# Sixteen key blocks of attention scores in six runs instead of seven, value products in groups of 4, 6 and 6

## The chip, the cores and the metric

The kernel runs on one core of one Trainium2 chip. The metric is the device time of one execution in microseconds (us); lower is better. TensorE (PE) does matrix products, ScalarE (ACT) exponentials and other table functions, VectorE (DVE) elementwise work, GpSimd (POOL) a few helpers; SyncE (SP) issues most DMAs. Each engine takes its own instructions in program order, and semaphores hold an instruction back until what it needs is there.

## The reference

The input x has 2048 tokens of 640 features. Two blocks read the same layer-normed xn, and their results are added to x:

```python
def _A_ref(x, wqkv, wo):              # H = 32 heads of Dh = 20
    q, k, v = qkv[0], qkv[1], qkv[2]  # from x @ wqkv
    scores = einsum("bhqd,bhkd->bhqk", q, k) * (Dh ** -0.5)
    p = _softmax(scores, axis=-1)
    o = einsum("bhqk,bhkd->bhqd", p, v)
    return o.transpose(...).reshape(B, S, D) @ wo

def _B_ref(x, w1, b1, w2, b2):        # F = 1536
    y = _layernorm(x, axis=-1)
    h = _gelu(y @ w1 + b1)
    return h @ w2 + b2

xn = _layernorm(x, axis=-1)
return x + _A_ref(xn, A_wqkv, A_wo) + _B_ref(xn, B_w1, B_b1, B_w2, B_b2)
```

## The kernel before

**Stages.** A first stage (to about 184 us of the profile) normalises x, projects queries, keys and a part of the values. The attention stage follows, and fills nearly all of the rest; what it leaves is the last part of the output projection.

**Tiles of the attention stage.** The heads go in 16 pairs, the queries in two halves of two chunks of 512. One pair and one chunk is a *tile* here; there are 64, numbered from 0, and each goes over 16 *key blocks* of 128 keys, numbered 0 to 15. For each block, `scores` (line 790) makes two matmuls side by side, one for each head of the pair, on 61 rows each, into one of three PSUM buffers, and ACT takes the exponential of the 128x1024 result into `p` (line 792). A next score waits until the exponential three blocks back has left its buffer.

**Value products.** `pv` (line 822) multiplies `p` by the values, four products of 32 columns side by side (a *wave*). A block goes in one of two ways, by the table `SPLIT`. For a 1, the upper 16 bits of `p` are multiplied as they are (one wave for a block), and the remainder, which DVE makes (`rest`, line 804, tile `low`), is multiplied in another wave for two blocks. For a 0 the float32 `p` is multiplied whole, two blocks in one wave of two passes. Inside a group the order is fixed:

```python
for kb, up, _ in split:                 # first the upper halves
    ...
for i in range(0, len(whole), 2):       # then the whole blocks, by twos
    ...
for i in range(0, len(split), 2):       # last the remainders, by twos
    for a in range(2):
        for n, (kb, _, low) in enumerate(split[i : i + 2]):
            product(2 * a + n % 2, vhalf, of16(kb, a), low[:, a])
```

So a group can't end before the remainder of its last split block is there.

**Other work.** Everything else that PE has to do (values, both layers of the second block, the output projection) is a generator `fill`, from which pieces are taken between the runs of scores: first-layer products `pu` (line 1083, a product is 30 matmuls and often falls in two pieces of 15), second-layer products `py` (line 1118), late values `pz`, projection `z`. After a `pu` product DVE and ACT compute the gelu: DVE lines 1014, 1016, 1018, 1020, then tanh on ACT (line 1025), then DVE lines 1027, 1028, 1029. The first of them, line 1014, reads `pu` and is issued with the last matmuls of the product; the others are issued at the following *ticks*, up to some 2 us of work in each. The row-sum divisions and their DVE lines 961 to 1004 (`finish`) come in ticks as well.

**The order.** It is written out by hand in `PLAN`: the rows are walked for each tile, and each word emits its work on all engines at that place.

- `s` the scores and the exponential of the next block
- `v4` or `v6` the value products of the oldest 4 or 6 blocks not yet multiplied (in the first row those are the previous tile's last 4)
- `l3` the remainder of block 3 on DVE, if the block is split
- `t`, `r` a tick (with `r`, tanh may be held back one tick)
- `m` a piece of other work, as much as the next number of `RATE` gives credit for
- `e` the copy of the previous tile's result out of PSUM on ACT (line 847)

After the second row the loads of the next tile's queries and keys are added to the ticks; they go on SP's queue.

Of the kernel before, what the change touches and what calls it, by code (L numbers as in the profile page):

```python
# [23 lines left out]
VW = DH + 1  # L24
PAD = 32 - VW
VROW = H * VW + PAD
SPLIT = (1, 1, 0, 0, 1, 1, 0, 0, 1, 1, 0, 0, 1, 1, 0, 0)
NPAIR = H // 2
EPS = 1e-5
TOP = 15.5  # L30
# [2 lines left out]
KROW = 32768.0  # L33
GRP = 4
CHUNK = 2.1
RATE = (2.0, 1.4, 2.2)
PLAN = ('s s t v4 l0 e', 's s l1 t s r m', 's s t v4', 's s l4 r l5 l8 m', 's s t l9 s r v4', 's l12 s m l13', 's r s v4')
UNITS = (3, 3, 3, 3, 2, 2)
ENDS = tuple(sum(UNITS[: i + 1]) for i in range(len(UNITS)))
TAIL = 12  # L40
# [8 lines left out]
def mha_mlp_kernel(tc, x, wqkv, wo, w1, b1, w2, b2, out):  # L49
# [4 lines left out]
    with (  # L54
# [124 lines left out]
        with tc.tile_pool(name="pa", bufs=2) as pa, tc.tile_pool(name="pa1", bufs=1) as pa1, tc.manual_schedule():  # L179
# [36 lines left out]
            for kb in range(NKB):  # L216
                if SPLIT[kb]:
                    nc.gpsimd.memset(V16[:, kb, :, DH : DH + 1], 1.0)
# [212 lines left out]
            def vproj_out(c, j, ps):  # L431
                kb = 4 * c + j
                pv_ = ps[:, :, :320].rearrange("p f (h d) -> p f h d", d=DH)
                vs = (V16 if SPLIT[kb] else V32)[:, kb].rearrange("p (f h) d -> p f h d", f=2)
                nc.scalar.activation(vs[:, :, :, :DH], pv_, AF.Copy, scale=2.0**-14)
                if SPLIT[kb]:
                    nc.vector.scalar_tensor_tensor(vs[:, :, :, VW : VW + DH], pv_, 2.0**-14, vs[:, :, :, :DH],
# [172 lines left out]
            def head_values(c, ps):  # L610

                for j in range(4):
                    kb = 4 * c + j
                    pv_ = ps[:, j // 2, j % 2 * VC :][:, :VC].rearrange("p (h d) -> p h d", d=DH)
                    vs = (V16 if SPLIT[kb] else V32)[:, kb, :VH]
                    nc.scalar.activation(vs[:, :, :DH], pv_, AF.Copy, scale=2.0**-14)
                    if SPLIT[kb]:
                        nc.vector.scalar_tensor_tensor(vs[:, :, VW : VW + DH], pv_, 2.0**-14, vs[:, :, :DH],
# [91 lines left out]
        with ExitStack() as scope:  # L710
# [88 lines left out]
            def rest(unit):  # L799

                kb, pt = unit[3:]
                if SPLIT[kb]:
                    low = ptp.tile([P, 2, 512], F16, tag="low", name="low", bufs=4)
# [486 lines left out]
            with tc.manual_schedule():  # L1290
# [15 lines left out]
                def other(turn):  # L1306

                    nonlocal credit
                    if not runs:
                        unit = next(fill)  # L1310
                        if unit is None:
                            credit = 0.0
                            return
                        n, cost = unit
                        lens, have = [], credit
                        while not lens or (cost - have > 0.5 * RATE[(turn + len(lens)) % len(RATE)] and len(lens) < n):
                            if lens:
                                have += RATE[(turn + len(lens)) % len(RATE)]
                            lens.append(max(0.0, have))
                        cuts = [round(n * v / lens[-1]) for v in lens] if lens[-1] > 0 else [n]  # L1320
                        runs.extend(y - x for x, y in zip([0] + cuts, cuts))
                    for _ in range(runs.pop(0)):
                        credit -= next(fill)

                for g, hf, cc in flow:
                    units = []
                    turn = 0
                    for r, steps in enumerate(PLAN):
                        for step in steps.split():
# [7 lines left out]
                            elif step == "m":  # L1337
                                credit += RATE[turn]
                                other(turn)
                                turn = (turn + 1) % len(RATE)  # L1340
                            elif step == "e":
# [5 lines left out]
                            else:  # L1347
                                now = int(step[1:])
                                if prev[0] is units[0] and r == 0:
                                    credit += RATE[0]  # L1350
                                    other(0)
# [121 lines left out]
```

## Time and profile before

| what | value |
|---|---|
| median of 3 runs | 1326.81 us (1326.32 to 1327.2) |
| span of the profiled execution | 1325.0 us |
| PE busy | 1313.6 us, 99% |
| ACT busy | 1117.6 us, 84% |
| DVE busy | 1067.1 us, 81% |

The span is the time from the first to the last instruction of the execution that the profiler recorded, so it is 1.8 us under the median of the runs; that execution's whole time is not given apart from its span. The page's busy shares are averages over the whole span. PE's matmuls overlap in the records, each with a modelled end, so the time that a run of matmuls costs is read as the distance from its first start to the next run's first start.

### The profile page before, as it was taken

How to read it: one execution, taken by the hardware profiler on the slowest of the kernel's cores; microseconds unless marked ns; L12 is line 12 of the kernel's file. 1: busy time of each engine (PE TensorE's matmuls, PEld its weight loads, DVE VectorE, ACT ScalarE, POOL GpSimd, SP SyncE). 2: the span in 40 equal slices, each digit the busy share in tenths (PEclk: the TensorE clock that was granted, in tenths of full speed). 3: DMA queues.
4: the chain of work that ended last, by engine and by line, in shares of the span. 5: the costliest groups of instructions: out<-in, count | busy, mean ns of one | idle time of the engine just before them, and what ended most of it. 6: DMA issues, size and time to landing. Idle time of an engine off the chain costs nothing.

```text
span 1325.0 us, 29048 instructions
## 1 busy us (share of the span) xinstructions
PE 1313.6 (99%) x11636; PEld 603.1 (46%) x11636; DVE 1067.1 (81%) x1450; ACT 1117.6 (84%) x1306; POOL 36.0 (3%) x84
## 2 busy tenths in 40 slices
PE   9999999999999999999999999999999999999998
PEld 6454564333444444444444444444444444444366
DVE  7668569798698987889988798998889899998742
ACT  7745369999999999999999999999999999999900
POOL 2000000000000000000000000000000000000000
PEclk9999999999999999999999999999999999999999
DMA  8697631121233321042312124132122333342376
GB/s 308 218 277 206 192 106 35 39 66 54 66 76 100 90 59 52 27 119 68 100 46 61 40 67 119 51 84 58 49 71 81 87 92 89 106 128 80 107 218 191
DMA packets 108166, 135.28 MB, mean 102 GB/s; under 512 B 24308, under 2 KB 74376, under 8 KB 107900
## 3 DMA queue, kind: packets, MB, share of 16 engines
q1 hardware_dynamic: 104588, 125.99, 31.6%
q0 software_dynamic: 2816, 6.90, 2.7%
q8 instruction: 92, 1.51, 0.5%
q10 hardware_dynamic: 624, 0.51, 0.1%
q14 instruction: 46, 0.38, 0.1%
HBM read 86.64 MB, written 43.74 MB: 98 GB/s over the span
## 4 chain that ended last, share of the span: by engine, by line
PE 90%; DVE 5%; ACT 3%; issue 1%; DMA 1%; SPq 0%; POOL 0%; ACTq 0%; DVEq 0%
PE o L822 31%; PE s L790 20%; PE py L1118 12%; PE pu L1083 12%; PE qkp L352 5%; PE z L1260 5%; PE pz L1162 2%; ACT p L792 2%; PE vp L425 1%; DVE st L263 1%; DVE qkhl L368 1%; ACT wv L476 1%; DVE xt L278 1%; ACT junk L101 0%; DVE low L804 0%
## 5 line engine op out<-in xcount | busy, mean ns | idle before, releaser
L792 ACT ACTIVATE p<-s 128x1024 f32<-128x1024 f32 x1024 | 967.9, 1047 | 55.1 <-PE s L790 53.0
L804 DVE TENSOR_TENSOR low<-p 128x1024 f16<-128x1024 f32 x512 | 610.5, 1220 | 123.1 <-ACT p L792 122.4
L822 PE MATMUL o<-p,vfull 128*32 128x512 bf16 (+1 forms) x4096 | 383.6, 493 | 0.0
L790 PE MATMUL s<-qs,ks 61*128 61x512 f16 x2048 | 304.4, 381 | 1.9 <-ACT p L792 1.3
L790 PEld LDWEIGHTS <-ks 61*128 61x128 f16 x2048 | 76.4, 94 | 237.0 <-issue 217.5
L1083 PE MATMUL pu<-xm,w1t 128*128 128x256 f16 x1440 | 172.3, 273 | 0.0
L1118 PE MATMUL py<-w2t,hT 128*128 128x320 f16 x1152 | 170.3, 300 | 1.2 <-DVE xb L1045 0.9
L1083 PEld LDWEIGHTS <-w1t 128*128 128x128 f16 x1440 | 133.8, 98 | 47.4 <-issue 33.0
L822 PEld LDWEIGHTS <-vfull 128*32 128x32 f16 x3072 | 60.1, 95 | 178.2 <-issue 178.0
L1118 PEld LDWEIGHTS <-hT 128*128 128x128 f16 x1152 | 106.3, 98 | 70.3 <-issue 32.6
L352 PE MATMUL qkp<-xnt,wv 128*128 128x512 f16 x600 | 131.4, 379 | 1.5 <-DVE qkhl L368 0.8
L822 PE MATMUL o<-low,vfull 128*32 128x512 f16 x1024 | 100.3, 378 | 0.0
L352 PEld LDWEIGHTS <-wv 128*128 128x128 f16 x600 | 58.1, 98 | 71.2 <-DVE qkhl L368 1.3
L822 PEld LDWEIGHTS o<-p,vfull 128*32 128x32 f32 x2048 | 61.5, 108 | 58.1
L1260 PE MATMUL z<-w1t,ot 128*128 128x320 f16 x480 | 66.9, 299 | 0.0
L1260 PEld LDWEIGHTS <-ot 128*128 128x128 f16 x480 | 46.2, 98 | 21.3 <-issue 3.7
L1217 DVE SCALAR_TENSOR_TENSOR acc<-z,sc,acc 128x320 f32<-128x320 f32 x32 | 17.6, 549 | 38.4 <-PE z L1260 37.6
L367 ACT ACTIVATE qkhl<-qkp,qks 128x1024 f16<-128x1024 f32 (+1 forms) x24 | 23.2, 965 | 29.5 <-PE qkp L352 18.8
L368 DVE SCALAR_TENSOR_TENSOR qkhl<-qkp,qks,qkhl 128x1024 f16<-128x1024 f32 (+1 forms) x24 | 26.5, 1105 | 25.4 <-ACT qkhl L367 25.3
L1108 POOL DMA_DIRECT2D xb<-in_B_b_dram x16 | 13.8, 863 | 1021.3 <-DMA xb<-in_A_x_dram 390.3
L847 ACT ACTIVATE ev<-o 128x512 f32<-128x512 f32 x64 | 38.6, 603 | 2.5 <-PE o L822 2.4
L1162 PE MATMUL pz<-hv,xm 128*128 128x480 f16 x180 | 39.9, 367 | 0.0
(205 smaller groups left out, 726.3 us busy)
## 6 DMA issues: line engine op xcount, KB each, us to landing
qkscr<-qkhl SPq DMA_DIRECT2D x40, 256.0 KB
opart<-ev SPq DMA_DIRECT2D x124, 80.0 KB
ks<-qkscr SPq DMA_DIRECT2D x120, 80.0 KB
xm<-xscr SPq DMA_DIRECT2D x13, 640.0 KB
qs<-qkscr SPq DMA_DIRECT2D x192, 40.0 KB
oa<-opart SPq DMA_DIRECT2D x32, 240.0 KB
xt<-in_A_x_dram SPq DMA_DIRECT2D x16, 320.0 KB
xscr<-xnt SPq DMA_DIRECT2D x4, 1280.0 KB
```

What stands on the lines that cost most here:

```text
L352: nc.tensor.matmul(ps[:, i, :], wv[:, k, q, a, mm * P : (mm + 1) * P], xnts[c][:, k, b, :], start=(k + n == 0), stop=(k == KD - 1 and n == 2))
L367: nc.scalar.activation(hl[:, 0, i0:i1], ps[:, i0:i1], AF.Copy, scale=a)
L368: nc.vector.scalar_tensor_tensor(hl[:, 1, i0:i1], ps[:, i0:i1], a, hl[:, 0, i0:i1], ALU.mult, ALU.subtract)
L790: nc.tensor.matmul(ps[:, a, :], ks[64 * a : 64 * a + 61, kb * P : (kb + 1) * P], qs[64 * a : 64 * a + 61, cc * 512 : (cc + 1) * 512], star ...
L792: nc.scalar.activation(pt, ps, AF.Exp, scale=QS)
L804: nc.vector.tensor_sub(low, pt, upper(pt))
L822: nc.tensor.matmul(pv.o[32 * q : 32 * q + 32, :], src[:, v0 - PAD * (1 - q % 2) :][:, :32], t, start=q not in pv.begun, stop=last, skip_gr ...
L847: nc.scalar.activation(evs[g, hf][:, cc], o, AF.Copy)
L1083: nc.tensor.matmul(ps[:, i], w1v[:, k, (f + i) // 4, a, fo_ : fo_ + P], xnt[:, k, b, :], start=(n == 0), stop=(n == 3 * KD - 1))
L1118: nc.tensor.matmul(ps[:, :320], hTs[mc][:, f, a, j * P : (j + 1) * P], w2v[:, f, b, hf * 320 : (hf + 1) * 320], start=(n == 0), stop=(n == ...
L1162: nc.tensor.matmul(ps[:, : D - VC], feats[c][:, k, a, j * P : (j + 1) * P], hv[:, k, b, :], start=(n == 0), stop=(n == 3 * KD - 1))
L1260: nc.tensor.matmul(ps[:, :320], ot[:, k, a, j * P : (j + 1) * P], wov[:, k, b, h * 320 : (h + 1) * 320], start=(n == 0), stop=(n == 3 * KD ...
```

## The change

Three tables of numbers change, and no line of the code that reads them:

```diff
-SPLIT = (1, 1, 0, 0, 1, 1, 0, 0, 1, 1, 0, 0, 1, 1, 0, 0)
+SPLIT = (1, 1, 0, 1, 1, 0, 1, 0, 0, 1, 0, 0, 1, 1, 0, 0)
...
-RATE = (2.0, 1.4, 2.2)
-PLAN = ('s s t v4 l0 e', 's s l1 t s r m', 's s t v4', 's s l4 r l5 l8 m', 's s t l9 s r v4', 's l12 s m l13', 's r s v4')
+RATE = (2.0, 1.5, 2.1)
+PLAN = ('s s t s v4 l0 e', 's l1 t s r m', 's l3 s t s l4 v6', 's s l6 t s r m', 's l9 t s v6', 's s l12 t s l13 m')
```

Scores go in runs of 3, 2, 3, 3, 2, 3 blocks instead of 2, 3, 2, 2, 3, 2, 2. Value products go in groups of 4 (the previous tile's blocks 12 to 15), 6 (blocks 0 to 5) and 6 (blocks 6 to 11) instead of four groups of 4. Eight blocks are split in both, but other ones: 0, 1, 3, 4, 6, 9, 12, 13 instead of 0, 1, 4, 5, 8, 9, 12, 13. A tile has three pieces of other work and eight ticks in both.

The first place is PE in tile 21, from the first remainders to the next scores. Before, the group ends with the remainders of blocks 0 and 1 (`low_6974`, `low_6987`):

```order
L822 LDWEIGHTS vfull_89
L822 MATMUL o_7026<-low_6974,vfull_89 32x512
L822 LDWEIGHTS vfull_89
L822 MATMUL o_7026<-low_6987,vfull_89 32x512
L822 LDWEIGHTS vfull_89
L822 MATMUL o_7026<-low_6974,vfull_89 32x512
L822 LDWEIGHTS vfull_89
L822 MATMUL o_7026<-low_6987,vfull_89 32x512
L790 LDWEIGHTS ks5_6335
L790 MATMUL s_7044<-qs5_6334,ks5_6335 128x512
```

Now, after the second head's remainders of blocks 0 and 1 (`low_6976`, `low_6984`), those of blocks 3 and 4 (`low_7019`, `low_7033`) stand ahead of the next scores:

```order
L822 MATMUL o_7035<-low_6976,vfull_89 32x512
L822 LDWEIGHTS vfull_89
L822 MATMUL o_7035<-low_6984,vfull_89 32x512
L822 LDWEIGHTS vfull_89
L822 MATMUL o_7035<-low_7019,vfull_89 32x512
L822 LDWEIGHTS vfull_89
L822 MATMUL o_7035<-low_7033,vfull_89 32x512
L822 LDWEIGHTS vfull_89
L822 MATMUL o_7035<-low_7019,vfull_89 32x512
L822 LDWEIGHTS vfull_89
L822 MATMUL o_7035<-low_7033,vfull_89 32x512
L790 LDWEIGHTS ks5_6335
```

The products with block 4's remainder moved one group forward: before, they stood in the tile's third group, after block 11's scores; now they stand before block 8's.

The second place is DVE in the same tile, from block 0's remainder on. Before, the remainders there are `low_6974` (block 0), `low_6987` (1), `low_7053` (4), `low_7056` (5):

```order
L1027 SCALAR_TENSOR_TENSOR u_6844<-w_6845,u_6844 128x512
L1028 TENSOR_SCALAR hT_5966<-u_6844,sc_91 128x2x256
L1029 SCALAR_TENSOR_TENSOR hT_5966<-u_6844,sc_91,hT_5966 128x2x256
L804 TENSOR_TENSOR low_6974<-p_6943 128x1024
L804 TENSOR_TENSOR low_6987<-p_6948 128x1024
L1014 TENSOR_TENSOR u_7011<-pu_6897,r2f_4261 128x512
L1016 TENSOR_TENSOR u_7011<-u_7011,b1t_94 128x512
L1018 TENSOR_TENSOR w_7012<-u_7011 128x512
L804 TENSOR_TENSOR low_7053<-p_6990 128x1024
L1020 SCALAR_TENSOR_TENSOR w_7012<-w_7012,u_7011 128x512
L804 TENSOR_TENSOR low_7056<-p_7014 128x1024
```

Now they are `low_6976` (block 0), `low_6984` (1), `low_7019` (3), `low_7033` (4):

```order
L804 TENSOR_TENSOR low_6976<-p_6942 128x1024
L804 TENSOR_TENSOR low_6984<-p_6947 128x1024
L1027 SCALAR_TENSOR_TENSOR u_6867<-w_6868,u_6867 128x512
L1028 TENSOR_SCALAR hT_5990<-u_6867,sc_91 128x2x256
L1029 SCALAR_TENSOR_TENSOR hT_5990<-u_6867,sc_91,hT_5990 128x2x256
L1014 TENSOR_TENSOR u_7011<-pu_6926,r2f_4289 128x512
L804 TENSOR_TENSOR low_7019<-p_6979 128x1024
L1016 TENSOR_TENSOR u_7011<-u_7011,b1t_94 128x512
L1018 TENSOR_TENSOR w_7012<-u_7011 128x512
L804 TENSOR_TENSOR low_7033<-p_6990 128x1024
```

The end of the previous gelu moved from ahead of block 0's remainder to behind block 1's, and the start of the next one now stands around block 3's remainder, ahead of block 4's. Nowhere does either kernel have more or fewer matmuls, exponentials or remainders than the other.

## Prediction, made before the changed kernel was run

> **What bounds the kernel now.** I read the page first, then PE's waits, then the long middle of the attention stage, then single tiles in the order of time.
>
> ```profile
> span 1325.0 us, 29048 instructions
> PE 1313.6 (99%) x11636; PEld 603.1 (46%) x11636; DVE 1067.1 (81%) x1450; ACT 1117.6 (84%) x1306; POOL 36.0 (3%) x84
> PEclk9999999999999999999999999999999999999999
> ...
> PE 90%; DVE 5%; ACT 3%; issue 1%; DMA 1%; SPq 0%; POOL 0%; ACTq 0%; DVEq 0%
> ```
>
> PE is busy 99% of the span and holds 90% of the chain that ended last. Who waits for whom:
>
> ```profile
> PE s L790 <- ACT p L792: 1.3, 5, 0.5
> DVE low L804 <- ACT p L792: 122.4, 121, 4.2
> ACT p L792 <- PE s L790: 53.0, 109, 2.1
> ```
>
> Columns are total us, times, longest. PE waits 1.3 us in the whole run for exponentials, and no row has it waiting for a remainder. ACT waits 53.0 us for scores: PE sets the pace. In the middle of the stage (busy us of PE, weight loads, DVE, ACT, POOL, then clock):
>
> ```profile
> 360.00:1150.00 790.00, 789.38 (x7462) 346.87 (x7455) 683.84 (x816) 748.88 (x843) 12.02 (x14) 1.00 0.27 74
> ```
>
> PE 789.4 of 790.0, ACT 748.9 (95%), DVE 683.8 (87%). So a tile gets shorter only if PE's own chain does, and ACT and DVE have 5% and 13% of room on average. Whether they have it at the moment at which PE asks is the question of this change.
>
> **What it takes away: switches.** These are PE's starts around two groups, some from narrow windows (start, then modelled length):
>
> ```profile
> 601.97 1.52 PE L1118 MATMUL py<-w2t,hT 128*128 128x320 f16 x10
> 603.42 0.61 PE L790 MATMUL s<-qs,ks 61*128 61x512 f16 x4
> 603.96 0.42 PE L822 MATMUL o<-p,vfull 128*32 128x512 bf16 x4
> 604.20 0.84 PE L822 MATMUL o<-p,vfull 128*32 128x512 bf16 x8
> 604.42 1.04 PE L822 MATMUL o<-p,vfull 128*32 128x512 f32 x8
> 604.85 0.61 PE L822 MATMUL o<-p,vfull 128*32 128x512 f32 x4
> 605.28 0.40 PE L822 MATMUL o<-low,vfull 128*32 128x512 f16 x4
> 605.61 0.61 PE L790 MATMUL s<-qs,ks 61*128 61x512 f16 x4
> ...
> 607.79 0.82 PE L790 MATMUL s<-qs,ks 61*128 61x512 f16 x6
> 608.55 2.35 PE L1118 MATMUL py<-w2t,hT 128*128 128x320 f16 x16
> ```
>
> Two blocks of scores cost 603.96 - 603.42 = 0.54, three 608.55 - 607.79 = 0.76: 0.22 for a block and 0.10 for each run. A group of 4 costs 605.61 - 603.96 = 1.65: upper waves 0.24 and 0.22, a whole wave 2 x 0.43, and 0.33 for the remainders, which is 0.11 over a block's 0.22, since the next matmul is of another kind. Per tile before: 16 x 0.22 + 7 x 0.10 + 4 x 1.65 = 10.82. After: 16 x 0.22 + 6 x 0.10 = 4.12; the group of 4, 1.65; blocks 0 to 5, four upper waves 3 x 0.24 + 0.22 = 0.94, one whole 0.86, two of remainders 0.22 + 0.33, together 2.35; blocks 6 to 11, 0.46 + 2 x 0.86 + 0.33 = 2.51. Sum 10.63. Saved: 0.19 a tile, 64 x 0.19 = 12 us.
>
> One price here is in no row: a wave of remainders behind another. Its bounds are 0.22 (a block inside its run) and 0.33 (as if kinds changed); the second would leave 64 x 0.08 = 5 us. I take 0.22, because two upper waves, the nearest row, follow at 0.24. [...]
>
> The other edits of this kind are worth nothing: three pieces of other work a tile with credit 5.6 both times, eight ticks both times, eight split blocks, the same DMAs behind the same second row. PE's work on them fills the same time wherever it is cut.
>
> **What it adds: a wait for block 4's remainder.** In the group of blocks 0 to 5 the second wave of remainders is due soon after the first piece of other work, and DVE has other instructions ahead of it. Tile 21 before:
>
> ```profile
> 540.43 0.85 PE L790 MATMUL s<-qs,ks 61*128 61x512 f16 x6
> 541.21 1.81 PE L1083 MATMUL pu<-xm,w1t 128*128 128x256 f16 x15
> 542.95 0.64 PE L790 MATMUL s<-qs,ks 61*128 61x512 f16 x4
> ...
> 543.06 0.69 DVE L1014 TENSOR_TENSOR u<-pu,r2f 128x512 f32<-128x512 f32 x1
> 543.78 0.69 DVE L1016 TENSOR_TENSOR u<-u,b1t 128x512 f32<-128x512 f32 x1
> 544.51 0.69 DVE L1018 TENSOR_TENSOR w<-u 128x512 f32<-128x512 f32 x1
> 545.12 1.22 DVE L804 TENSOR_TENSOR low<-p 128x1024 f16<-128x1024 f32 x1
> 546.25 0.68 DVE L1020 SCALAR_TENSOR_TENSOR w<-w,u 128x512 f32<-128x512 f32 x1
> ```
>
> The piece ends at 542.95; call it R. Line 1014 starts 0.11 later, as soon as `pu` is there. The steps on DVE, start to start: 0.72 for 1014, 0.73 for 1016, 0.61 for 1018, 1.13 for a remainder, whose result is there after 1.22. After the change the order is 1014, block 3's remainder, 1016, 1018, block 4's: done at R + 0.11 + 0.72 + 1.13 + 0.73 + 0.61 + 1.22 = R + 4.52. PE wants it at R + 0.76 (three scores) + 0.94 + 0.86 + 0.22 = R + 2.78. It waits 1.74 us, and behind it, on PE's queue, stand block 8's scores: ACT runs dry, having only blocks 5 to 7 to work off. Before, the same remainder was due six blocks of scores later; its lateness cost nothing. That cover is gone.
>
> The order of DVE's instructions sorts the 64 tiles:
>
> - 13 tiles are like this: 13 x 1.74 = 22.6 us.
> - In 8 tiles (the changed tile 21 is one) the end of an earlier gelu also stands ahead of 1014. For it and for the time at which block 1's remainder is done, rows of other tiles:
>
> ```profile
> 621.88 0.60 PE L790 MATMUL s<-qs,ks 61*128 61x512 f16 x4
> 623.39 2.36 DVE L804 TENSOR_TENSOR low<-p 128x1024 f16<-128x1024 f32 x2 [1.72 <-ACT p L792]
> 625.67 0.22 DVE L961 TENSOR_TENSOR lt<-lt 96x64 f32<-96x64 f32 x1
> ...
> 656.03 0.69 DVE L1027 SCALAR_TENSOR_TENSOR u<-w,u 128x512 f32<-128x512 f32 x1
> 656.76 0.49 DVE L1028 TENSOR_SCALAR hT<-u,sc 128x512 f16<-128x512 f32 x1
> 657.28 0.75 DVE L1029 SCALAR_TENSOR_TENSOR hT<-u,sc,hT 128x512 f16<-128x512 f32 x1
> 657.95 2.35 DVE L804 TENSOR_TENSOR low<-p 128x1024 f16<-128x1024 f32 x2
> ...
> L998 DVE TENSOR_TENSOR oa<-oa 120x512 f32<-120x512 f32 x16 | 11.0, 685 | 0.0
> ```
>
>   With T the tile's first score, DVE is free of block 1's remainder at 625.67, T + 3.79, and of the gelu's end, 657.95 - 656.03 = 1.92 long, at T + 5.71. R is T + 0.76 + 1.65 + 0.54 + 1.74 = T + 4.69. So 1014 starts 1.02 after R and not 0.11: a wait of 2.65, 8 x 2.65 = 21.2. In six of them one or two of the `finish` lines (0.69 each) stand there too: + 5, together 26.
> - In 4 tiles the gelu's end, which must wait for tanh, stands between the remainders of blocks 3 and 4. At least 1.1 (nothing late but DVE's own lines), at most the 2.65 above; I take 2.0: 8 us.
> - In 14 tiles the gelu's end stands ahead of block 3's remainder and no 1014 follows: block 4's is done at T + 5.71 + 1.13 + 1.22 = T + 8.06, and PE, after a `py` piece of 14 (about 2.0, between the 1.45 of 10 and the 2.28 of 16), is there at T + 7.73. Some 0.4 each, and one or two `finish` lines in half of them: 12 us.
> - In the other 25, and in the third group of all, which needs block 11's exponential one run after its scores, waits run from nothing to about 1 us (0 to 25 in all); I take 12, half.
>
> Together 80.6 us of waits less 12 saved: + 68. The span becomes 1325.0 + 68 = 1393, the time 1395 with the 1.8 us by which the median lies above this span.
>
> **Rivals.**
>
> *The waits don't come, and the switches are saved: 1315 us.* It is so if DVE's remainders are ready when PE comes, and turns at an average wait of 0.19 us a tile. For it: PE waits for none before, and DVE has 13% free. Against it: 4.52 against 2.78 needs no load at all, only the order of five instructions. Chance 4%.
>
> *ACT becomes the bound as well: 1420 us.* Only block 12's scores stand between block 11's and the group that needs its exponential. ACT's room is 41 us in the 790 above; if the third group waits 0.4 us in every tile, 64 x 0.4 = 26 come on top of the forecast. Against it: PE's new waits stand earlier in each tile, and give ACT time to catch up. Chance 9%.
>
> *PE's clock falls after the longer waits: 1415 to 1450 us.* The granted clock is 9 in every slice and 1.00 in the middle, but PE had no pause there to show what one does. If what follows a wait (three scores and a piece, 0.76 + 1.74 = 2.5) took double, that is 20 us for the 8 longest and 53 for 21. [...] Chance 5%.
>
> That PE and DVE don't take the new order is not open: each takes its instructions as they stand.
>
> **How the numbers follow.** The forecast has 82%, the rivals 4, 9 and 5. Slower therefore 95%, faster 4%, and 1% for within 0.2% (2.7 us, about what a measurement of this kernel can tell from no change). The low end of the range: only the waits that DVE's order forces, 22.6 + 21.2 + 4 x 1.1 = 48, less 13: 1362. The high end: all of the 25 for the last kind (+ 13), 5 saved and not 12 (+ 7): 1415; I go to 1360 and 1420, into the second and third rival.
>
> **What would show it.** The waits of PE should have a row on `o` of line 822 for DVE `low` of line 804 with 60 to 90 us in all and 3 to 4.5 at the longest; PE falls to about 95% busy; ACT's idle time for scores rises from 53 us to well over 100. A three-block run must still cost 0.76 and the two big groups without a wait 2.35 and 2.51. I am wrong if block 4's remainder is done by R + 2.8, or if the waits lie on exponentials.

## The result and the profile after

The changed kernel takes 1427.24 us (median of 4 runs, 1425.41 to 1430.78) against 1327.01 us before (4 runs): a ratio of 1.0758, with a 95% interval of 1.074 to 1.0775. That is 100 us more; 68 were forecast, and 1427 lies above the range, which ended at 1420.

The page of the profile after: span, busy time, granted clock, and the chain by engine and by line.

```profile
span 1426.4 us, 28903 instructions
PE 1341.5 (94%) x11636; PEld 629.8 (44%) x11636; DVE 1071.2 (75%) x1450; ACT 1118.3 (78%) x1306; POOL 36.5 (3%) x84
PEclk9999999999999999999999999999999999999999
...
PE 51%; DVE 23%; ACT 17%; issue 6%; DMA 2%; SPq 1%; ACTq 0%; POOL 0%; DVEq 0%
PE o L822 16%; ACT p L792 13%; DVE low L804 11%; PE s L790 9%; PE py L1118 8%; PE qkp L352 6%; PE z L1260 5%; PE pu L1083 4%; DVE u L1014 2%; DVE u L1016 2%; DVE w L1018 2%; PE pz L1162 1%; ACT ev L847 1%; PE vp L425 1%; DVE hT L1029 1%
```

PE is down from 99% to 94% busy. On the chain, 90% PE has become 51%, and DVE and ACT hold 40%. The work of ACT and DVE is the same as before within 5 us. The waits (total us, times, longest):

```profile
PE o L822 <- DVE low L804: 38.2, 37, 2.7
PE s L790 <- ACT p L792: 35.1, 95, 0.6
ACT p L792 <- PE s L790: 154.2, 155, 3.7
```

Two waits of PE have grown from next to nothing and are about equally large: for a remainder, as forecast, and for exponentials ahead of the *scores*, which was not. The two rows hold 73 us, and the loss is 100. A matmul's end is modelled, and a wait that lies under the modelled end of the matmul before is not counted. So the sums below go *by starts*: the distance from the first start of a run of scores, or of a group, to the first start of what comes next, less the smallest such distance at that place, added up over the 64 tiles.

| place in the tile | waits before | waits after |
|---|---|---|
| first run of scores | 0.0 | 21.7 |
| third run of scores (after: blocks 5 to 7) | 2.8 | 35.2 |
| all other runs of scores | 6.3 | 2.3 |
| group of blocks 0 to 5 | - | 51.4 |
| group of blocks 6 to 11 | - | 9.8 |
| all groups of 4 | 1.6 | 0.3 |
| sum, us | 10.7 | 120.7 |

Tile 21 after the change has both waits. PE in the order of time (start, modelled length, in brackets the visible idle time before):

```profile
574.44 0.61 PE L790 MATMUL s<-qs,ks 61*128 61x512 f16 x4
575.28 0.39 PE L790 MATMUL s<-qs,ks 61*128 61x512 f16 x2 [0.23 <-ACT p L792]
575.60 1.52 PE L822 MATMUL o<-p,vfull 128*32 128x512 bf16 x16
...
577.80 1.81 PE L1083 MATMUL pu<-xm,w1t 128*128 128x256 f16 x15
579.55 0.79 PE L790 MATMUL s<-qs,ks 61*128 61x512 f16 x4
580.86 0.39 PE L790 MATMUL s<-qs,ks 61*128 61x512 f16 x2 [0.52 <-ACT p L792]
581.18 1.96 PE L822 MATMUL o<-p,vfull 128*32 128x512 bf16 x24
582.96 0.59 PE L822 MATMUL o<-low,vfull 128*32 128x512 f16 x5
584.89 0.40 PE L822 MATMUL o<-low,vfull 128*32 128x512 f16 x3 [1.34 <-DVE low L804]
585.22 0.82 PE L790 MATMUL s<-qs,ks 61*128 61x512 f16 x6
585.98 2.62 PE L1118 MATMUL py<-w2t,hT 128*128 128x320 f16 x18
```

The run of three from 574.44 lasts 1.16 and the one from 579.55 lasts 1.63, where 585.22 to 585.98 shows the price of one that doesn't wait, 0.76. The group from 581.18 lasts 4.04 where 2.31 would do, because its second wave of remainders (584.89) comes late. DVE and ACT at the same time:

```profile
579.70 0.75 DVE L1029 SCALAR_TENSOR_TENSOR hT<-u,sc,hT 128x512 f16<-128x512 f32 x1
580.55 0.69 DVE L1014 TENSOR_TENSOR u<-pu,r2f 128x512 f32<-128x512 f32 x1
581.16 1.22 DVE L804 TENSOR_TENSOR low<-p 128x1024 f16<-128x1024 f32 x1
582.29 0.69 DVE L1016 TENSOR_TENSOR u<-u,b1t 128x512 f32<-128x512 f32 x1
583.01 0.69 DVE L1018 TENSOR_TENSOR w<-u 128x512 f32<-128x512 f32 x1
583.62 2.35 DVE L804 TENSOR_TENSOR low<-p 128x1024 f16<-128x1024 f32 x2
...
577.42 1.06 ACT L792 ACTIVATE p<-s 128x1024 f32<-128x1024 f32 x1
578.33 0.65 ACT L847 ACTIVATE ev<-o 128x512 f32<-128x512 f32 x1
578.80 4.75 ACT L792 ACTIVATE p<-s 128x1024 f32<-128x1024 f32 x5
```

Block 4's remainder starts at 583.62 and takes 1.22; PE goes on at 584.89, 5.34 after the piece's end at 579.55. The forecast for such a tile was 1.02 - 0.11 + 4.52 = 5.43. As to the scores, ACT starts block 3's exponential at 578.80, behind the copy of the previous result (line 847). Block 4's follows some 0.9 later and takes about 1.06, to 580.8, and that is when block 7's scores get their buffer (580.86).

### The profile page after: what moved, and what is told of

It is laid out like the page before. It is cut to its first block, busy times and chain, and to the rows that moved or that the text cites. A ratio compares the mean times of both kernels' runs of the same rounds, so it can differ in the third digit from the quotient of the medians.

```text
span 1426.4 us, 28903 instructions
## 1 busy us (share of the span) xinstructions
PE 1341.5 (94%) x11636; PEld 629.8 (44%) x11636; DVE 1071.2 (75%) x1450; ACT 1118.3 (78%) x1306; POOL 36.5 (3%) x84
## 4 chain that ended last, share of the span: by engine, by line
PE 51%; DVE 23%; ACT 17%; issue 6%; DMA 2%; SPq 1%; ACTq 0%; POOL 0%; DVEq 0%
PE o L822 16%; ACT p L792 13%; DVE low L804 11%; PE s L790 9%; PE py L1118 8%; PE qkp L352 6%; PE z L1260 5%; PE pu L1083 4%; DVE u L1014 2%; DVE u L1016 2%; DVE w L1018 2%; PE pz L1162 1%; ACT ev L847 1%; PE vp L425 1%; DVE hT L1029 1%
## 5 line engine op out<-in xcount | busy, mean ns | idle before, releaser
L822 PE MATMUL o<-p,vfull 128*32 128x512 bf16 (+1 forms) x4096 | 378.4, 493 | 0.6 <-ACT p L792 0.6
L790 PE MATMUL s<-qs,ks 61*128 61x512 f16 x2048 | 310.7, 381 | 36.0 <-ACT p L792 35.1
L790 PEld LDWEIGHTS <-ks 61*128 61x128 f16 x2048 | 82.0, 94 | 246.2 <-issue 218.6
L822 PEld LDWEIGHTS <-vfull 128*32 128x32 f16 x3072 | 72.6, 96 | 210.2 <-issue 190.2
L1083 PEld LDWEIGHTS <-w1t 128*128 128x128 f16 x1440 | 134.4, 98 | 51.4 <-issue 36.6
L822 PE MATMUL o<-low,vfull 128*32 128x512 f16 x1024 | 109.2, 380 | 38.3 <-DVE low L804 38.2
L822 PEld LDWEIGHTS o<-p,vfull 128*32 128x32 f32 x2048 | 69.4, 108 | 82.5 <-issue 25.7
L1014 DVE TENSOR_TENSOR u<-pu,r2f 128x512 f32<-128x512 f32 x48 | 33.1, 689 | 36.5 <-PE pu L1083 35.5
L1027 DVE SCALAR_TENSOR_TENSOR u<-w,u 128x512 f32<-128x512 f32 x48 | 33.0, 688 | 16.6 <-ACT w L1025 16.6
```

What stands on the lines that cost most here:

```text
L790: nc.tensor.matmul(ps[:, a, :], ks[64 * a : 64 * a + 61, kb * P : (kb + 1) * P], qs[64 * a : 64 * a + 61, cc * 512 : (cc + 1) * 512], star ...
L822: nc.tensor.matmul(pv.o[32 * q : 32 * q + 32, :], src[:, v0 - PAD * (1 - q % 2) :][:, :32], t, start=q not in pv.begun, stop=last, skip_gr ...
L1014: nc.vector.tensor_mul(u, ps, r2f[:, None, :].to_broadcast([P, 2, MC]))
L1027: nc.vector.scalar_tensor_tensor(u, w, 1.0, u, ALU.add, ALU.mult)
L1083: nc.tensor.matmul(ps[:, i], w1v[:, k, (f + i) // 4, a, fo_ : fo_ + P], xnt[:, k, b, :], start=(n == 0), stop=(n == 3 * KD - 1))
```

## The experiments

Two theories. **1:** PE waits for block 4's remainder, which stands behind the gelu on DVE; the rest are small change. **2:** ACT limits the runs. There are three PSUM buffers, so the third score of a run of three has to wait until ACT has finished the last exponential of the run before. Now there are four such runs in a tile, and before there were two. Where no interval is given, a kernel was run once; runs of the changed kernel lie up to 5.4 us apart.

**Remainders of other blocks.** The products with the remainders of blocks 3 and 4 read those of blocks 0 and 1 instead, which are there long before; DVE still makes all eight. The edit acts only where a group has more than two remainders, the group of blocks 0 to 5:

```diff
                         for n, (kb, _, low) in enumerate(split[i : i + 2]):
+                            low = split[n][2]
                             product(2 * a + n % 2, vhalf, of16(kb, a), low[:, a])
```

> The changed kernel, but in the group of blocks 0 to 5 the products with the remainders of blocks 3 and 4 read those of blocks 0 and 1, which are long there; DVE still makes all eight. Theory 1 (PE waits for block 4's remainder, which stands behind the gelu on DVE): in the changed kernel that group lasts 199.1 us in all against 147.8 without a wait, so some 51 us of waits; without them, and with a few us left for block 5's exponential, 1380 to 1390. Theory 2 (it is ACT: three-block runs come too close for three PSUM buffers, and the remainders only show what ACT delays): the waits move to the scores, 1410 or more.

Measured: 1379.4 us, 48 less than the changed kernel and 0.6 below the range of theory 1.

```profile
PE s L790 <- ACT p L792: 35.0, 95, 0.6
PE o L822 <- DVE low L804: 3.4, 6, 0.6
```

The wait for the remainder is gone (the group of blocks 0 to 5 keeps 3.2 us), and the row of the scores stays to 0.1 us. The waits did not move there: the two are separate. Theory 1 holds for half of the loss.

**Half of the exponentials.** ACT takes the exponential of one head's half of each block only, and both heads use it:

```diff
-                nc.scalar.activation(pt, ps, AF.Exp, scale=QS)
+                nc.scalar.activation(pt[:, 0], ps[:, 0], AF.Exp, scale=QS)
...
-                    nc.vector.tensor_sub(low, pt, upper(pt))
+                    nc.vector.tensor_sub(low, pt[:, 0:1].to_broadcast([P, 2, 512]),
+                                         upper(pt)[:, 0:1].to_broadcast([P, 2, 512]))
```

and `up[:, 0]`, `pt[:, 0]` for `[:, a]` in the products.

> The changed kernel, but ACT takes the exponential of one head's 512 columns of each block instead of 1024, and value products and remainders read that half for both heads; PE's and DVE's instructions and sizes stay. Theory 2 (the third score of a run waits for its PSUM buffer, 22 us in a tile's first run and 35 us in its third): both waits go, the remainder's in the 25 tiles with a gelu in the way stays (about 13 x 1.7 + 8 x 2.7 + 4 x 2): 1365 to 1385. Theory 1 alone: less than 12 us gained, 1415 or more.

Measured: 1378.6 us, 49 less. Of the two rows only one is left (line 823 is line 822 of the changed kernel, moved by the edit):

```profile
PE o L823 <- DVE low L804: 50.1, 43, 2.7
```

By starts, all waits of scores are gone (about 1 us left in 64 tiles). The group of blocks 0 to 5 now waits 68.1 us in place of 51.4: PE comes to it earlier and DVE is hardly sooner done. So theory 2 holds for the other half.

**Both.**

> Both edits at once. If the two waits are all that the change costs, nothing is left but the saved switches: 1305 to 1315, under the kernel before. If something else was paid (the half clock in three windows of 3.4 us, loads that come late, a dearer group of six), it stays above 1327.

Measured: 1319.5 us, 108 less than the changed kernel; the kernel before took 1328.4 us on the same chip. It is 4.5 us above what was expected: 12.5 us of waits are left in the third group, about 8 of them for block 9's remainder and 4 for block 11's exponential. So waits of these two kinds are the loss, and below them the change does save. How much, the next one shows.

**The kernel before with half of the exponentials** (the same edit).

> The kernel before, with the exponentials of one head's half only, as in the run of the changed kernel with half exponentials. It shows what the kernel before would take if PE never waited for ACT: its scores wait some 9 us in all, so 1316 to 1320. Together with the run of both edits (1319.5, of which 12.5 us are waits left in the third group) it gives the saved switches alone: if they are 12 us as forecast, this run lies at or below 1320; if the bigger groups save nothing, it lies near 1307.

Measured: 1320.3 us (4 runs; ratio to the kernel before 0.9941, 0.9927 to 0.9956). From the first score to the end of the last group this run takes 1073.2 us and the changed kernel with both edits 1073.3, but with about 4 and 16 us of waits in it. The runs of scores and the groups alone add up, without their waits, to 688 and 674 us: the change saves 14 us of PE's time. 12 were forecast.

**The tick behind the group.** One word of the changed kernel moves:

```diff
-PLAN = (..., 's l3 s t s l4 v6', ...)
+PLAN = (..., 's l3 s s l4 v6 t', ...)
```

> The changed kernel with one word moved: in PLAN's third row the tick goes behind the group of six. Then lines 1016 and 1018 follow block 4's remainder on DVE, not the other way round; line 1014 still comes first. Theory 1: block 4's remainder is done 0.11 + 0.72 + 1.13 + 1.22 = 3.2 us after the piece, against 4.5, and the third score of the run is late by some 0.4 anyway: of 1.74 in each of 13 tiles about 0.4 stays, of 2.7 in 8 about 1.3: 1393 to 1405. If the gelu's place is not the cause: 1420 or more.

Measured: 1387.3 us, 40 less, and better than expected by 6 us.

```profile
PE s L790 <- ACT p L792: 35.0, 95, 0.6
PE o L822 <- DVE low L804: 8.7, 14, 0.8
```

By starts, the wait of the group of blocks 0 to 5 falls from 51.4 to 15.0 us, and those of the scores stay (21.7 and 35.1). 28 of the 36 us were in the 21 tiles in which lines 1016 and 1018 stood between the remainders of blocks 3 and 4. There the place of two gelu lines in DVE's order made block 4's remainder late, not DVE's load, which is nearly the same (1068.6 us busy, 1071.2 in the changed kernel).

**Other split blocks.** The changed kernel with

```diff
-SPLIT = (1, 1, 0, 1, 1, 0, 1, 0, 0, 1, 0, 0, 1, 1, 0, 0)
+SPLIT = (1, 1, 0, 0, 0, 0, 1, 1, 1, 1, 0, 0, 1, 1, 0, 0)
-PLAN = (..., 's l3 s t s l4 v6', 's s l6 t s r m', 's l9 t s v6', ...)
+PLAN = (..., 's s t s v6', 's s l6 t s l7 r l8 m', 's l9 t s v6', ...)
```

> The changed kernel with other split blocks (0, 1, 6, 7, 8, 9, 12, 13), so that the group of blocks 0 to 5 needs no late remainder; blocks 6 and 7 are made in the fourth row, 8 at its end, 9 in the fifth. Theory 1: the second group loses its waits (about 48 us, as with other remainders), the third keeps or gains some: 1378 to 1392. If a remainder is late wherever four of them are due in one group: 1400 or more.

Measured: 1394.3 us, 33 less and just above the range. The second group has no wait to speak of (1.7 us). The third, in which all of blocks 6 to 9 now need a remainder, has 21.8 in place of 9.8, measured from its own smallest distance, 2.46; a group with as many remainders took 2.31 in the changed kernel, and from there it is 31. The scores' waits stay to 0.1 us (21.7 and 35.1).

**Long pieces ahead of the runs that wait.** The tick behind the group, and

```diff
-RATE = (2.0, 1.5, 2.1)
+RATE = (2.4, 0.9, 2.3)
```

> The kernel with the tick behind the group (1387.3), and the credit of the three pieces 2.4, 0.9, 2.3 in place of 2.0, 1.5, 2.1, so that longer pieces stand ahead of the two runs of three whose third score waits (57 us in all). Theory 2a (the wait is only a matter of the gap ahead of the run): of the 57 about 30 go, 1355 to 1365. Theory 2b (ACT has no room: before a run of three it must have run dry, four times a tile, and work is only moved): what those runs gain, the run of two behind the short piece loses: 1375 to 1395.

Measured: 1398.1 us, 11 more than without it. The first run's waits fall from 21.7 to 9.3 us and the third's from 35.1 to 16.5, as theory 2 has it. But the fifth run, of two, behind the short piece, goes from 0.9 to 24.6, and the two groups of six from 26.6 together to 42.6. All waits together rise from 85 to 95 us: they were moved, not taken away. That is what theory 2b said, though the time ended 3 us above its range.

**The copy on DVE.** The tick behind the group, and the copy of a tile's result out of PSUM, which ACT makes just ahead of block 3's exponential, on DVE:

```diff
-                        nc.scalar.activation(evs[g, hf][:, cc], o, AF.Copy)
+                        nc.vector.tensor_copy(evs[g, hf][:, cc], o)
```

> The kernel with the tick behind the group (1387.3), and the copy of a tile's result out of PSUM made by DVE instead of ACT. It takes ACT 0.5 us a tile, just ahead of block 3's exponential, on which the third run's last score waits (35 us in all). Theory 2 (ACT's lag at that place is the wait): most of the 35 goes, 1355 to 1368; DVE may make block 0's or 1's remainder later, which is due only 5 us on. If the buffers' count and not ACT's lag sets that wait: 1380 or more.

Measured: 1400.6 us, 13 more than without it, where 20 to 32 less were expected.

```profile
PE o L822 <- DVE low L804: 28.3, 49, 1.1
PE s L790 <- ACT p L792: 17.2, 54, 0.5
```

The mechanism was right: by starts the third run's waits fall from 35.1 to 9.6 us, and the first run's stay at 21.7. But the copy, 0.7 us on DVE, stands between the remainders of blocks 0 and 1, and all behind it come later. The group of blocks 0 to 5 waits 50.2 us in place of 15.0, 0.55 more a tile. That block 1's remainder is due much later was true and beside the point; block 4's, behind it, is not.

**The kernel before, two small parts.** The changed RATE alone:

> The kernel before with the changed RATE alone (second piece 1.5 in place of 1.4, third 2.1 in place of 2.2). Of its 9 us of waits 3.5 are in the run of three behind the second piece; a longer piece there takes 1 to 2 of them away: 1324 to 1327, 0.9975 to 1.000 of the time before. It can't be the cause of any of the 100 us.

Measured: 1.0007 (0.9998 to 1.0015) of the time before, no difference; waits of 1 us went from one run of scores to another. And the copy on DVE:

> The kernel before with the same copy on DVE. PE's waits there are some 9 us for ACT, and the kernel with half exponentials, which had none of them, took 1320.3: between 1320 and 1328. If DVE's remainders come late for it, 1330 or more.

Measured: 1.0008 (0.9999 to 1.0017), no difference. Both were expected a little lower. No version that was run beats the kernel before with the whole computation in it.

## Why the prediction was wrong

The sign and the first mechanism were right; the size was not, and a second mechanism was missing. A *switch* is what PE loses where it goes from one kind of product to another, and the *gelu's end* is DVE's lines 1027 to 1029. By the terms of the prediction's sum:

| term | forecast | measured, by starts |
|---|---|---|
| switches saved | -12 | -14 |
| 13 tiles with a `pu` end ahead of block 3's remainder | 22.6 | 22.7 |
| 8 tiles with a gelu's end as well | 26 | 24.3 |
| 4 tiles with it between blocks 3 and 4 | 8 | 10.4 |
| 14 tiles with it ahead of block 3 | 12 | 11.3 |
| the other 25, and the third group of all | 12 | 17.9 + 9.8 |
| first run of scores | not there | 21.7 |

Here a tile's third run and second group are taken together, since what a late remainder costs doesn't depend on where PE stood before. In the 13 tiles that sum is between 1.7 and 1.9 in each; 1.74 was the forecast. The run with half of the exponentials has the remainder's wait alone: 1.71 in each of the 13 tiles (22.3 in all), and 22.8, 9.7 and 8.6 us in the next three rows. So the forecast of the remainder held. In the row of the 14 tiles the agreement is luck: 7.9 of its 11.3 us are waits of scores.

Two sizes of the prediction can be checked as well. A second wave of remainders follows the first at 0.22 us, as was assumed (first starts at 364.328 and 364.543), and the group of blocks 0 to 5 lasts 2.31 without a wait, where the sum had 2.35. The low end of the range takes off 13 us where the sum saves 12.

**The step that failed** is the wait of the scores for ACT, which was put at nothing. In the sum it shows in two places: the last term, "the other 25, and the third group", where 27.7 us stand against 12 and 13.7 of them are waits of scores, and the first run, 21.7 us, for which there was no term. I worked out when the *remainders* come, for each kind of tile, and never when the *scores* may start. The rows were there: a score needs the exponential three blocks back, and the forecast used the price of a run of three that doesn't wait, 0.76, for every run. For the first run the sum would have been as follows. A run of three (0.76), a piece of 1.74, and two more blocks of scores (0.44) bring the third score at 2.94 after the previous run's start. But ACT starts 0.45 after a run's first score (558.52 against 558.07 below), and that run's third exponential ends at 0.45 + 2 x 0.91 + 1.03 = 3.3. That is a wait of 0.4 in each tile with such a piece, and more with a shorter one; the table has 21.7 for the 64. The third run, behind the copy on ACT, waited 0.55 a tile on average. The kernel before could have told: its scores waited in the run of three behind the second piece too, 3.5 us in 64 tiles, and I read the 1.3 us on the waits' page as nothing, without asking what hides under modelled ends. The prediction's own sign of being wrong, waits that lie on exponentials, came true for half of the loss.

**The rivals.** The second named ACT, with 9%, and its time, 1420, was the nearest. But its place was wrong for the most part: it had the third group wait for block 11's exponential. That happened in some 15 tiles and cost about 4 us; its price, 26 us, came from an assumed 0.4 in every tile. What waits in nearly all tiles is the third score of a run for its buffer. "ACT's room is 41 us" was read as room, but the room is not where the runs ask for it. This is ACT through tile 20 of the profile after (the bracket is its idle time; the run of blocks 0 to 2 starts on PE at 558.07):

```profile
558.52 2.86 ACT L792 ACTIVATE p<-s 128x1024 f32<-128x1024 f32 x3 [0.41 <-PE s L790]
561.25 0.62 ACT L847 ACTIVATE ev<-o 128x512 f32<-128x512 f32 x1
561.73 4.72 ACT L792 ACTIVATE p<-s 128x1024 f32<-128x1024 f32 x5
566.84 4.69 ACT L792 ACTIVATE p<-s 128x1024 f32<-128x1024 f32 x5 [0.38 <-PE s L790]
572.37 3.78 ACT L792 ACTIVATE p<-s 128x1024 f32<-128x1024 f32 x4 [0.85 <-PE s L790]
```

ACT stands ahead of the exponentials of blocks 0, 8 and 13, and not ahead of block 5's. PE's run of blocks 0 to 2 has no wait here, that of blocks 5 to 7 has 0.6 us. In all 64 tiles of the changed kernel:

| run of three | ACT idle ahead of its first exponential, us | waits of its scores, us |
|---|---|---|
| blocks 0 to 2 | 10.9 | 21.7 |
| blocks 5 to 7 | 0.9 | 35.2 |
| blocks 8 to 10 | 69.5 | 0.9 |
| blocks 13 to 15 | 65.3 | 0.1 |

Where ACT had run dry, PE's run of three went without a wait; where it had not, PE waited. Ahead of block 0 it holds tile by tile: ACT stood in 19 tiles (0.39 us or more), and none of their runs waited; of the other 45, 42 did. So ACT stood for 135 us at two places of the tile, and PE lost 57 at the two others. (Ahead of block 8 much of it is the late group of blocks 0 to 5: in the run with other remainders 21.3 us are left there.) The kernel before had 53 us of such idle time in all, 0.8 a tile. The pieces and the copy that were moved only shifted the waits. Whether another order with six runs could use ACT's idle time was not tried.

A third cause would have been possible: eight blocks' `p` (0 to 7) are now in use before the group of blocks 0 to 5, and the pool has seven buffers, so block 7's exponential has to wait for block 0's products. It cost nothing: ACT has no idle time ahead of block 7's exponential in any of the 64 tiles.

The first rival (nothing waits, 1315 us) is close to what the run with both edits shows, 1319.5. The third assumed that what follows a wait takes double, in 8 or 21 places, and no row of before shows that. In the changed kernel it came about at three places, for at most 5 us (below).

## What to carry to other kernels

A longer run on the bounding engine saves a switch, here 0.1 us each, but it asks for all buffers at once, here for 57 us of waits: before lengthening runs, add up for each run when the oldest buffer comes free, not whether the consumer has room on average. When a group of products is made larger, its last operand is due earlier, and here the group of blocks 0 to 5 waited 51.4 us; look at what stands ahead of that operand in its producer's order, for one instruction of another chain is enough: one copy of 0.7 us a tile on DVE raised a group's waits from 15.0 to 50.2 us. And the totals of the wait rows were too low here, 73 us where the starts show 121, since ends are modelled; the distance between starts, less the smallest such distance, is the better measure, as long as some tile doesn't wait at that place.

## What the hardware showed that was not expected

While PE had work, its granted clock fell to 0.50 three times, each time for 3.41 us (from 216.08, 714.42 and 1229.83), behind a pause. The window, its length, busy us of PE, weight loads, DVE, ACT and POOL, then the clock, and last the DMA's share and GB/s:

```profile
212.00:216.07 4.07, 1.25 (x13) 0.40 (x9) 4.04 (x5) 0.52 (x1) 0.00 (x0) 1.00 0.00 0
216.08:219.48 3.40, 3.40 (x18) 1.79 (x16) 2.12 (x3) 3.36 (x4) 0.00 (x0) 0.50 0.00 0
219.50:223.00 3.50, 3.50 (x38) 1.05 (x34) 3.10 (x4) 2.03 (x3) 0.00 (x0) 1.00 0.02 5
714.43:717.83 3.40, 3.40 (x15) 1.91 (x14) 2.49 (x4) 2.71 (x4) 0.00 (x0) 0.50 0.00 0
1229.84:1233.24 3.40, 3.40 (x15) 1.41 (x14) 2.19 (x3) 2.91 (x4) 0.00 (x0) 0.50 0.59 189
```

Twelve `pu` matmuls took 2.68 us in the first stretch, start to start, and 1.41 from 207.76 on, at a clock of 1.00. The pauses ahead of the stretches, start to start, are 2.5, 2.1 and 3.1 us; two others of 2.1 and 2.2 us were followed by no such stretch. The length of the pause doesn't settle it: in the run with long pieces (mean granted clock 0.999) one of 2.95 us had none behind it, and in the run with the copy on DVE after the tick (0.997) a stretch at 1202.77 followed 3.40 us in which PE was busy for 1.57, with no wait above 1.1. What does settle it was not shown. At most half of 3 x 3.41 us, 5 of the 100 us, can come from it, an estimate that has everything in a stretch take twice its time. The page's row of the clock shows nothing of it: a slice is 36 us, and its digit stays 9.
